# State part of a delta-rule kernel's outputs: one 96-column matmul over both heads of a pair, or one per head over 48 rows

## The chip, the cores and the metric

The kernel runs on one core of one Trainium2 chip. The metric is the time of the device for one execution, in microseconds (us), median of several runs. The engines are TensorE (PE, its weight loads are listed apart as PEld), VectorE (DVE), ScalarE (ACT), GpSimd (POOL) and SyncE (SP, which issues all transfers here).

## What is computed

A delta-rule recurrence over 768 positions for 4 batches of 8 heads with 48 features each, whose output goes through two feed-forward layers (384 to 2048 to 384) with different pointwise functions:

```python
for t in range(S):
    y[:, :, t] = np.einsum('bhd,bhde->bhe', q[:, :, t], state)
    v_old = np.einsum('bhde,bhd->bhe', state, kt)
    state = state + bt[:, :, :, None] * np.einsum('bhd,bhe->bhde', kt, vt - v_old)
x = y.transpose(0, 2, 1, 3).reshape(B * S, H * D)     # 3072 x 384
h = x @ w_in                                          # layer 1
x = np.where(h > 0, h, np.exp(np.minimum(h, 0)) - 1) @ w_out
h = x @ w_in2                                         # layer 2
x = ((a0 + a1*h + a2*h*h + a3*h*h*h) / (1 + |b0|*|h| + |b1|*h*h + 1e-6)) @ w_out2
```

## The kernel before, in words

The recurrence is cut into 12 chunks of 64 positions; two chunks make a window, six windows in all (w = 0 to 5). Within a chunk the 32 pairs of batch and head are handled as 16 pairs of heads: the two heads of a pair lie on partitions 0 to 47 and 64 to 111. A chunk has two halves (hf = 0, 1) of eight head pairs each. Its steps, each a group of PE matmuls in fp32 with copies behind it, are: gp (products of keys and queries, into the masked matrix p), ks (keys times state), a triangular solve in three groups (solve with tp_t, lo, solve with tp_t again), whose result is copied into ub (128 tokens of two batches, 8 pairs, 2 heads, 48 features), yy (the outputs), ku (the update of the state s_bd) and xx (transposes of the outputs into xs, the input of layer 1).

The function yy (line 1007) makes the outputs of one half in one PSUM tile y of 128 x 384. For a chunk that is not the first it issues eight matmuls of the state part, `lhsT` 128 x 64 from kq and `rhs` 128 x 96 from s_bd. s_bd is block diagonal: rows 0 to 47 hold the first head's state in columns 0 to 47, rows 64 to 111 the second's in columns 48 to 95, and the rest is zero. Then it issues eight matmuls of the other part, `lhsT` 128 x 64 from p, `rhs` 128 x 96 from ub, and they are added in PSUM to the first eight. The 64 output rows are tokens; two batches (bl = 0, 1) go to PSUM partitions 0 to 63 and 64 to 127 in turn. One ACT copy brings y to y1 in SBUF (for the first chunk DVE does it). The loads of later chunks (ch_ahead) are called from yy (kq) and ku (kv). xx (line 1030) transposes y1 and copies it into xs; when both chunks of a window are through, split_x (line 911) splits xs into a coarse and a fine part, xh and xl, for layer 1.

Layer 1 and 2 are groups of nine matmuls of 128 x 512 (kind "F" here: H for the first product, O for the second; 2.04 us each). The chain of window w + 1 is issued among the F groups of window w. After window 5 come only F groups, until the end.

The order is not written out by hand. All operations are recorded first (class Recorder), with group kinds for PE (`rc.brk("yy")`). Then `order` (line 329) plans them: `simulate` (line 350) plays the program with estimated durations (PEC, LEAVE, ENTER, PAIR: ns per matmul and ns from the start of one group to the next by kind), margins (SLACK) and tie-breaks drawn from numbers (MIX); the best of eight rounds gives the order in which each engine's instructions are emitted. Each engine then runs its list in that order and waits on semaphores. The times at which the steps are recorded (`chain`, line 921, with SLOTS) set the rank of the groups. The chain's matmuls write to PSUM tiles of the pool pa, three tiles that go round in the order of recording. Where PE would be idle before the first F group, `gaps` (line 314) fills in matmuls without use ("fill").

fp32 matmuls appear in the trace as two MATMUL rows each, with a LDWEIGHTS row each. All recorded operations carry line 191 in the profile (the recorder's emit), so groups are told apart by their tiles.

Of the kernel before, what the change touches and what calls it, by code (L numbers as in the profile page):

```python
# [10 lines left out]
F32 = mybir.dt.float32  # L11
# [3 lines left out]
AF = mybir.ActivationFunctionType  # L15
# [5 lines left out]
D = 48  # L21
NSC = 12
NF = 16
DM = 384
# [7 lines left out]
Q = dict(  # L32
    ma=-200, xo=2.244, pg0=0, pg1=2, ca=0, g1=-72.135, g1d=1.259, t1a=-33.632, t1b=-8, npre=24, ta=-5, tb=4, hd=0.4, c0=-47,
    c0d=1.9, c1=-1.042, c1r=3.6, b1=0.704, c1o=0.919, h0=1.013, h0d=0.5, h1=0.586, h1d=0.462, g2=-7.824,
    g2d=1.116, g3w1=-0.578, g3=-0.806, t2=2.578, t2b=14.166, t3b=9, p=14.315, tm=4, chd=1.061, ws=0.808,
    sx=-0.529, ev=16.5, c5=1.1, c5d=0.4, l5=1.3, wu0=0, wl0=2, wd0=5, wy0=2, wm0=2, wu1=6, wl1=7, wd1=6, wy1=0,
    wm1=6, wk=4, wr=3, wr0=4)
# [135 lines left out]
class Recorder:  # L173
# [58 lines left out]

    def mm(self, out, lhsT, rhs, start, stop):
        kind = self.group.kind
        pitch, lat = PEC[kind]
        self.add("PE", self.nc.tensor.matmul, dict(out=out, lhsT=lhsT, rhs=rhs, start=start, stop=stop), [out], [lhsT, rhs], pitch, lat)

    def transpose(self, out, in_, ident):
# [2 lines left out]
    def act(self, out, in_, **kw):  # L241
        n = out.ids.size
        d = 200 + n * .833 - (30 if in_.base.psum else 0)
        extra = [x for x in kw.values() if isinstance(x, View)]
        d += 90 * len(extra)
        self.add("ACT", self.nc.scalar.activation, dict(out=out, in_=in_, **kw), [out], [in_] + extra, d + self.gap(out, 100), d)
# [4 lines left out]
    def dma(self, out, in_):  # L251
        v = out if isinstance(out, View) else in_
        n = v.ids.size * 4 * (v.part[1] - v.part[0])
        self.add("SP", self.nc.sync.dma_start, dict(out=out, in_=in_), [out], [in_], SLACK["issue"], 2000, n)

# [41 lines left out]

PEC = {
    "F": (226.7, 425), "gp": (206, 475), "ks": (22, 330), "so": (31, 220), "lo": (22, 250), "yy": (85, 262), "ku": (47, 263),
    "xx": (90, 405), "wm": (200, 500), "yt": (33, 260)}  # L300
LEAVE = {"F": 2040, "so": 1062, "lo": 812, "ks": 804, "gp": 914, "ku": 855, "yy": 1471, "xx": 290, "wm": 500, "yt": 1400}
ENTER = {"F": 0, "so": 71, "ks": 71, "xx": -25, "ku": 70, "yy": 20, "gp": -20, "lo": 100, "wm": 50, "yt": 20}
PAIR = {
# [3 lines left out]
SIZE = {"F": 9, "yy": 16, "yt": 48}  # L307
SLACK = {"small": 0, "F": 200, "x": 30, "issue": 500, "rate": 240, "land": 2300, "wait": 1500, "space": 3900, "room": 290, "first": 432, "hold": 200, "jit": 800, "pj": 40}
MIX = [
    (97143513, 1), (80976384, 3), (2505799, 200), (79334811, 200), (73314090, 200), (46793208, 200),  # L310
    (69792616, 200), (68619154, 200), (27185215, 200), (40519137, 200), (78123636, 200), (916308, 200),
]


# [7 lines left out]
def mixed(n):  # L322
    for seed, share in MIX[:0:-1]:
        if draw(seed + 1, n) * share < 1.0:
            return draw(seed, n)
    return draw(MIX[0][0], n)


def order(ops, rounds):
    groups = []  # L330
    for o in ops:
        if o.group is not None and o.group.ops[0] is o:
            o.group.n = o.n
            o.group.rank = o.n + (0 if o.group.kind == "F" else SLACK["pj"] * (mixed(o.n) - .5))
            groups.append(o.group)
            t = 0
            for m in o.group.ops:
                m.off = t
                t += m.pitch
        o.late, o.tie = o.n, mixed(o.n)  # L340
    mine = {o: None for o in ops}
    for o in ops:
        o.deps = {d: k for d, k in o.deps.items() if d in mine}
        for d in o.deps:
            d.succ.append(o)
    best = None
    for _ in range(rounds):
        end = simulate(ops)
        if best is None or end < best[0]:
            best = end, {o: o.start for o in ops}  # L350
        backward(ops, end)
    for o, s in best[1].items():
        o.start = s
    return best[0], sorted(ops, key=lambda o: (o.start, o.n))
# [19 lines left out]
def pe_cost(a, b):  # L374
    return PAIR.get((a, b), LEAVE[a] + ENTER[b])


def simulate(ops):
# [31 lines left out]
    def finish(o, t):  # L410
        nonlocal end
        end = max(end, t)
        for s in o.succ:
# [7 lines left out]
            if g is not None:  # L421
                gready[g] = max(gready[g], r - s.off + SLACK["F" if g.kind == "F" else "small"])
                gleft[g] -= 1
                if not gleft[g]:
                    push(g, gready[g])
            else:
                s.ready = max(s.ready, r + (0 if o.eng == s.eng else SLACK["x"]))
                s.left -= 1
# [3 lines left out]
    def issue(u, t, k):  # L432
# [3 lines left out]
        for o in u.ops:  # L436
            t0 = t + o.off * k + shift
            count += q
            if count > SLACK["first"] - SLACK["room"] + 254.6 * len(usable):
                asked = max(t0 + SLACK["wait"], asked + SLACK["space"])  # L440
                usable.append(asked + 2450)
# [112 lines left out]
def kernel(  # L554
# [16 lines left out]
    nc = tc.nc  # L571
    rc = Recorder(nc)
    mm, act, vector, gpsimd = rc.mm, rc.act, Recorder.Eng(rc, "DVE", nc.vector), Recorder.Eng(rc, "POOL", nc.gpsimd)
    NW = len(WINS)

    def pool(stack, name, bufs, **kw):
        return Pool(rc, stack.enter_context(tc.tile_pool(name=name, bufs=bufs, **kw)), bufs, kw.get("space") is PSUM)
# [18 lines left out]
    ap2 = pool(p1, "ap2", 2)  # L596
    pa = pool(p1, "pa", 3, space=PSUM)
# [23 lines left out]
    p_d = {}  # L621
    s_bd = ap1.tile([128, 16, 2, D], F32, name="s_bd")
# [141 lines left out]
    def ch_ahead(nm):  # L764
        if ch_n[nm] < len(ch_q):
            s, hf = ch_q[ch_n[nm]]
            if nm == "kq":
                t = ap2.tile([128, 8, 128], F32, tag="kq", name="kq")
                rc.dma(out=t, in_=c_kq[s, hf])
            else:  # L770
                t = ap2.tile([128, 8, 96], F32, tag="kv", name="kv")
                rc.dma(out=t, in_=c_kv[s, hf])
            ch_t[nm, s, hf] = t
            ch_n[nm] += 1
# [125 lines left out]
    def warm(dep, n):  # L900
        return
        t = wt.get(0)
        if t is None:
            t = wt[0] = po.tile([128, 512], F32, tag="o0", name="warm")
        rc.brk("wm")
        mm(out=t[0:dep.shape[-1], 0:64 * n], lhsT=dep, rhs=p_d[0][0:dep.shape[0], 0:n].rearrange("p a b -> p (a b)"), start=True, stop=True)
# [14 lines left out]
    def chain(w, slots=SLOTS):  # L921
# [8 lines left out]
        for j, s in enumerate(WINS[w]):  # L930
            st = [dict(), dict()]
# [75 lines left out]
            def yy(hf, j=j, s=s, st=st):  # L1007
                d = st[hf]
                y = pa.tile([128, DM], F32, tag="pa", name="y")
                rc.brk("yy")  # L1010
                if s > 0:
                    for u in range(8):
                        bl, i = u % 2, u // 2
                        mm(out=y[64 * bl:64 * bl + 64, 96 * i:96 * i + 96], lhsT=d["kq"][:, 4 * bl + i, 64 * bl:64 * bl + 64],
                           rhs=s_bd[:, 8 * hf + 4 * bl + i].rearrange("p a b -> p (a b)"), start=(i == 0), stop=False)
                    ch_ahead("kq")
                for u in range(8):
                    bl, i = u % 2, u // 2
                    if w == 0 and u == 4:
                        warm(d["ub"][:, 0, 0, 0:16], Q[f"wm{j}"])  # L1020
                        rc.brk("yy")
                    mm(out=y[64 * bl:64 * bl + 64, 96 * i:96 * i + 96], lhsT=p_d[s][:, 8 * hf + 4 * bl + i],
                       rhs=d["ub"][:, 4 * bl + i].rearrange("p a b -> p (a b)"), start=(s == 0), stop=(s == 0 or i == 3))
                y1 = d["y1"] = ap2.tile([128, DM], F32, tag="y1", name="y1")
                if s == 0:
                    vector.tensor_copy(out=y1, in_=y)
                else:
                    act(out=y1, in_=y, func=AF.Copy)
# [30 lines left out]
            def mk(*fs):  # L1059
                def f():  # L1060
                    for fn, hf in fs:
                        fn(hf)
                return f

            if j == 0:
                xs_d[w] = box
            sl = slots[j]
            items += [
                (sl[0], mk((prep, 0))), (sl[1], mk((prep, 1))), (sl[2], mk((ks, 0), (ks, 1))),
                (sl[3], u1), (sl[4], lo), (sl[5], u2),  # L1070
                (sl[6], mk((yy, 0))), (sl[8], mk((yy, 1))),
                (sl[6] + Q["xo"], mk((xx, 0))), (sl[8] + Q["xo"], mk((xx, 1)))]
            if not last:
                items += [(sl[7], mk((ku, 0))), (sl[9], mk((ku, 1)))]
# [357 lines left out]
    _, first = order(rc.ops, 8)  # L1432
# [94 lines left out]
```

## Time and profile before

| | us |
|---|---|
| median of 3 runs | 1018.04 (1017.91 to 1019.07) |
| the profiled execution | 1017.7 |
| its span, first to last instruction | 1015.9 |
| PE busy | 1001.9 (99%) |
| DVE, ACT, POOL busy | 870.4 (86%), 746.4 (73%), 388.3 (38%) |
| mean granted clock of TensorE | 0.996 |

Busy times are unions over the span. PE rows are pipelined: a MATMUL row lasts longer than the distance to the next one, so distances between starts tell more than durations. The stretch from about 88 to 583 us is layer 1 with the chains of windows 1 to 5 in between; before it lies the chain of window 0, behind it layer 2.

### The profile page before, as it was taken

To read this page: it belongs to the slowest core of one execution; us is meant where nothing else is said; L and a number is where in the kernel's file an instruction comes from. 1 tells how busy PE (TensorE), PEld (TensorE's weight loads), DVE (VectorE), ACT (ScalarE), POOL (GpSimd) and SP (SyncE) were. 2 spreads that over 40 slices of the span, in tenths; PEclk is the share of its full clock that TensorE was granted. 3 is DMA by queue.
4 is the path that set the end of the run, shared out by engine and by line. 5 is a ranking of instruction groups with operands and counts; after the bars stand their busy time and mean duration, and the time that the engine had idled before them with its cause. 6 is when DMAs were issued, how large, how long until landed. Compare 5 with 4: busy or idle time off the path is not lost.

```text
span 1015.9 us, 23204 instructions
## 1 busy us (share of the span) xinstructions
PE 1001.9 (99%) x9234; PEld 833.6 (82%) x9234; DVE 870.4 (86%) x1314; ACT 746.4 (73%) x1467; POOL 388.3 (38%) x287
## 2 busy tenths in 40 slices
PE   8999999999999999999999999999999999999997
PEld 7877888888888888888878888888888888888885
DVE  4999988995997799599875677999999999999996
ACT  4569899877777786778778878677676776766763
POOL 1253655642322223213222235363363553633332
PEclk9999999999999999999999999999999999999999
DMA  9745284217524542642155973001010010000000
GB/s 265 207 139 174 72 239 124 85 62 229 166 76 131 171 166 60 218 152 76 56 173 160 317 244 105 21 10 53 1 63 1 1 63 1 31 1 1 32 1 31
DMA packets 66956, 106.07 MB, mean 104 GB/s; under 512 B 7840, under 2 KB 40736, under 8 KB 66848
## 3 DMA queue, kind: packets, MB, share of 16 engines
q1 hardware_dynamic: 66848, 104.59, 32.7%
q8 instruction: 72, 1.18, 0.5%
q14 instruction: 36, 0.29, 0.1%
HBM read 82.55 MB, written 22.02 MB: 103 GB/s over the span
## 4 chain that ended last, share of the span: by engine, by line
PE 88%; DVE 4%; DMA 3%; ACT 3%; issue 1%; SPq 0%; DVEq 0%; ACTq 0%
PE o L191 37%; PE h L191 18%; PE h_b L191 10%; PE h_a L191 9%; PE cb L191 3%; PE gp L191 3%; PE y L191 2%; PE ku L191 2%; PE ks L191 1%; DMA gin<-g_in 1%; ACT wo L191 1%; PE h_c L191 1%; DMA xg<-g_in 1%; PE xt L191 1%; DVE wo L191 1%; DVE tmp L191 1%
## 5 line engine op out<-in xcount | busy, mean ns | idle before, releaser
L191 POOL TENSOR_TENSOR wor<-wo,wor 128x384 fp32r<-128x384 f32 x96 | 115.6, 1207 | 269.5 <-ACT wor L191 256.7
L191 POOL TENSOR_TENSOR gl<-wo 128x1024 fp32r<-128x1024 f32 x47 | 141.1, 3002 | 191.4 <-DVE wo L191 155.4
L191 PE MATMUL o<-gh,wor 128*128 128x512 f32 x576 | 194.7, 396 | 0.0
L191 PE MATMUL h<-xh,wi 128*128 128x512 f32 x546 | 183.7, 395 | 0.2 <-issue 0.2
L191 ACT ACTIVATE wo<-wo 128x1024 f32<-128x1024 f32 (+3 forms) x224 | 143.0, 671 | 37.2 <-DVE wo L191 34.1
L191 PE MATMUL o<-gh,wo 128*128 128x512 f32 x576 | 139.7, 391 | 0.0
L191 PEld LDWEIGHTS o<-gh,wo 128*128 128x128 f32 x576 | 108.8, 189 | 22.7
L191 PEld LDWEIGHTS o<-gh,wor 128*128 128x128 f32 x576 | 108.1, 188 | 23.1
L191 PEld LDWEIGHTS h<-xh,wi 128*128 128x128 f32 x546 | 102.5, 188 | 22.2 <-ACT pe L191 0.3
L191 PE MATMUL o<-gl,wor 128*128 128x512 f32 x288 | 112.3, 390 | 0.0
L191 PE MATMUL h<-xl,wi 128*128 128x512 f32 x273 | 106.6, 391 | 0.2 <-DVE xl L191 0.2
L191 DVE SCALAR_TENSOR_TENSOR wo<-wo 128x192 int32<-128x192 int32 (+2 forms) x101 | 88.0, 875 | 16.2 <-ACT wo L191 16.1
L191 DVE SCALAR_TENSOR_TENSOR e<-e,pe 128x512 f32<-128x512 f32 x96 | 74.7, 778 | 30.7 <-ACT e L191 30.2
L191 PE MATMUL h_b<-xh,wi 128*128 128x512 f32 x300 | 96.4, 389 | 0.0
L191 DVE TENSOR_TENSOR gl<-e,gh 128x512 fp32r<-128x512 f32 x88 | 73.6, 836 | 18.7 <-ACT gh L191 18.4
L191 PE MATMUL h_a<-xh,wi 128*128 128x512 f32 x276 | 88.9, 389 | 0.0
L191 ACT ACTIVATE wo<-h_b,ab_sb 128x1024 f32<-128x1024 f32 (+1 forms) x52 | 57.6, 1129 | 35.3 <-PE h_b L191 32.8
L191 ACT ACTIVATE e<-h 128x512 f32<-128x512 f32 x91 | 54.4, 598 | 35.5 <-PE h L191 33.9
L191 PE MATMUL o<-gl,wo 128*128 128x512 f32 x288 | 73.8, 391 | 2.0 <-DVE gl L191 2.0
L191 ACT ACTIVATE gh<-e 128x512 fp32r<-128x512 f32 x96 | 60.7, 632 | 15.7 <-PE o L191 10.1
L191 DVE SCALAR_TENSOR_TENSOR gh<-wo,ab_sb 128x1024 fp32r<-128x1024 f32 (+1 forms) x49 | 63.3, 1291 | 9.0 <-ACT wo L191 3.5
L191 PEld LDWEIGHTS h_b<-xh,wi 128*128 128x128 f32 x300 | 56.3, 188 | 11.7
(126 smaller groups left out, 2098.5 us busy)
## 6 DMA issues: line engine op xcount, KB each, us to landing
gin<-g_in SPq DMA_DIRECT2D x69, 192.0 KB, 4.2
kq<-c_kq SPq DMA_DIRECT2D x22, 512.0 KB, 4.7
kv<-c_kv SPq DMA_DIRECT2D x24, 384.0 KB, 5.8
raw<-w_out SPq DMA_DIRECT2D x42, 192.0 KB, 3.0
raw<-w_in SPq DMA_DIRECT2D x34, 192.0 KB, 3.6
o2d<-cs SPq DMA_DIRECT2D x32, 192.0 KB, 2.7
i2d<-cs SPq DMA_DIRECT2D x32, 192.0 KB, 2.3
wi<-i2d SPq DMA_DIRECT2D x16, 384.0 KB, 3.9
```

Source lines behind the costliest of these rows:

```text
L191: fn(**{k: v.real() if isinstance(v, View) else v for k, v in kw.items()})
```

## The change

For windows 1 to 5 a new function yb replaces the two calls of yy: one group (kind "yz") with both halves of the chunk. It has two PSUM tiles, one for each head of a pair, each 128 x (2 halves, 4 pairs, 48). The state part is multiplied per head: `lhsT` 48 x 64 and `rhs` 48 x 48, on partitions from 0 or from 64, 32 matmuls a chunk where there were 16 of 128 x 64 by 128 x 96. The other part has `rhs` 128 x 48 per head, 32 matmuls where there were 16 with 96 columns. Four ACT copies of 128 x 192 (half and head) bring the two tiles to the two y1 tiles, where two copies of 128 x 384 did. Both kq loads of the chunk are called behind the group's matmuls. Window 0 keeps yy; its second call is now recorded at the first one's place, and the break within its group is gone. The planner gets constants for "yz", a lookup by the number of rows, other margins and other numbers for its tie-breaks.

```diff
--- before.py
+++ after.py
@@ -232,7 +232,7 @@
 
     def mm(self, out, lhsT, rhs, start, stop):
         kind = self.group.kind
-        pitch, lat = PEC[kind]
+        pitch, lat = PEC.get((kind, lhsT.part[1] - lhsT.part[0]), PEC[kind])
         self.add("PE", self.nc.tensor.matmul, dict(out=out, lhsT=lhsT, rhs=rhs, start=start, stop=stop), [out], [lhsT, rhs], pitch, lat)
 
     def transpose(self, out, in_, ident):
@@ -297,18 +297,19 @@
 
 PEC = {
     "F": (226.7, 425), "gp": (206, 475), "ks": (22, 330), "so": (31, 220), "lo": (22, 250), "yy": (85, 262), "ku": (47, 263),
-    "xx": (90, 405), "wm": (200, 500), "yt": (33, 260)}
-LEAVE = {"F": 2040, "so": 1062, "lo": 812, "ks": 804, "gp": 914, "ku": 855, "yy": 1471, "xx": 290, "wm": 500, "yt": 1400}
-ENTER = {"F": 0, "so": 71, "ks": 71, "xx": -25, "ku": 70, "yy": 20, "gp": -20, "lo": 100, "wm": 50, "yt": 20}
+    "xx": (90, 405), "yz": (22, 262), ("yz", 128): (43, 262),  "wm": (200, 500), "yt": (33, 260)}
+LEAVE = {"F": 2040, "so": 1062, "lo": 812, "ks": 804, "gp": 914, "ku": 855, "yy": 1471, "yz": 2200, "xx": 290, "wm": 500, "yt": 1400}
+ENTER = {"F": 0, "so": 71, "ks": 71, "xx": -25, "ku": 70, "yy": 20, "yz": 20, "gp": -20, "lo": 100, "wm": 50, "yt": 20}
 PAIR = {
-    ("F", "so"): 2131, ("F", "gp"): 2140, ("F", "lo"): 2263, ("F", "yy"): 2266, ("F", "ks"): 2225, ("F", "xx"): 2049,
+    ("F", "so"): 2131, ("F", "gp"): 2140, ("F", "lo"): 2263, ("F", "yy"): 2266, ("F", "yz"): 2266, ("F", "ks"): 2225, ("F", "xx"): 2049,
     ("F", "ku"): 2230, ("F", "yt"): 2266, ("ks", "ks"): 704, ("yy", "yy"): 1371, ("yy", "ku"): 1371, ("yy", "xx"): 1421, ("yy", "gp"): 1435,
     ("ku", "ku"): 755, ("ku", "yy"): 755, ("xx", "ku"): 450, ("xx", "ks"): 477, ("yt", "yt"): 1365}
 SIZE = {"F": 9, "yy": 16, "yt": 48}
-SLACK = {"small": 0, "F": 200, "x": 30, "issue": 500, "rate": 240, "land": 2300, "wait": 1500, "space": 3900, "room": 290, "first": 432, "hold": 200, "jit": 800, "pj": 40}
+SLACK = {"small": 150, "F": 100, "x": 15, "issue": 500, "rate": 240, "land": 2000, "wait": 2000, "space": 3900, "room": 290, "first": 432, "hold": 200, "jit": 800, "pj": 0}
 MIX = [
-    (97143513, 1), (80976384, 3), (2505799, 200), (79334811, 200), (73314090, 200), (46793208, 200),
-    (69792616, 200), (68619154, 200), (27185215, 200), (40519137, 200), (78123636, 200), (916308, 200),
+    (52832997, 1), (92410015, 200), (32312298, 200), (83369229, 200), (2388703, 200), (46334073, 60),
+    (81258500, 60), (36371637, 200), (64931058, 200), (82440171, 200), (11413780, 60), (11428128, 200),
+    (90112574, 200), (20237250, 20),
 ]
 
 
@@ -1016,11 +1017,33 @@
                     ch_ahead("kq")
                 for u in range(8):
                     bl, i = u % 2, u // 2
-                    if w == 0 and u == 4:
-                        warm(d["ub"][:, 0, 0, 0:16], Q[f"wm{j}"])
-                        rc.brk("yy")
                     mm(out=y[64 * bl:64 * bl + 64, 96 * i:96 * i + 96], lhsT=p_d[s][:, 8 * hf + 4 * bl + i],
                        rhs=d["ub"][:, 4 * bl + i].rearrange("p a b -> p (a b)"), start=(s == 0), stop=(s == 0 or i == 3))
+                y_out(y, d, s)
+
+            def yb(_, s=s, st=st):
+                rc.brk("yz")
+                ys = [pa.tile([128, 2, 4, D], F32, tag="pa", name="y") for _ in range(2)]
+                for i in range(4):
+                    for bl in range(2):
+                        for hf, d in enumerate(st):
+                            for h in range(2):
+                                rs = slice(64 * h, 64 * h + D)
+                                mm(out=ys[h][64 * bl:64 * bl + 64, hf, i], lhsT=d["kq"][rs, 4 * bl + i, 64 * bl:64 * bl + 64],
+                                   rhs=s_bd[rs, 8 * hf + 4 * bl + i, h], start=(i == 0 and hf == 0), stop=False)
+                for hf, d in enumerate(st):
+                    for i in range(4):
+                        for h in range(2):
+                            for bl in range(2):
+                                mm(out=ys[h][64 * bl:64 * bl + 64, hf, i], lhsT=p_d[s][:, 8 * hf + 4 * bl + i], rhs=d["ub"][:, 4 * bl + i, h],
+                                   start=False, stop=(hf == 1 and i == 3))
+                for hf, d in enumerate(st):
+                    ch_ahead("kq")
+                    y1 = d["y1"] = ap2.tile([128, DM], F32, tag="y1", name="y1")
+                    for h in range(2):
+                        act(out=y1.rearrange("p (i h d) -> p i h d", h=2, d=D)[:, :, h], in_=ys[h][:, hf], func=AF.Copy)
+
+            def y_out(y, d, s):
                 y1 = d["y1"] = ap2.tile([128, DM], F32, tag="y1", name="y1")
                 if s == 0:
                     vector.tensor_copy(out=y1, in_=y)
@@ -1068,7 +1091,7 @@
             items += [
                 (sl[0], mk((prep, 0))), (sl[1], mk((prep, 1))), (sl[2], mk((ks, 0), (ks, 1))),
                 (sl[3], u1), (sl[4], lo), (sl[5], u2),
-                (sl[6], mk((yy, 0))), (sl[8], mk((yy, 1))),
+                (sl[6], mk((yy, 0), (yy, 1)) if w == 0 else mk((yb, 0))),
                 (sl[6] + Q["xo"], mk((xx, 0))), (sl[8] + Q["xo"], mk((xx, 1)))]
             if not last:
                 items += [(sl[7], mk((ku, 0))), (sl[9], mk((ku, 1)))]
```

## Rows read from the trace of the kernel before

**Rows 1.** The page, part 1: busy us (share of span) x instructions

```profile
PE 1001.9 (99%) x9234; PEld 833.6 (82%) x9234; DVE 870.4 (86%) x1314; ACT 746.4 (73%) x1467; POOL 388.3 (38%) x287
```

**Rows 2.** Busy us of each engine, PEclk, DMA share, GB/s, one stretch

```profile
265.00:353.00 88.00, 87.76 (x1229) 73.77 (x1232) 75.34 (x156) 68.58 (x165) 25.04 (x21) 1.00 0.47 147
```

**Rows 3.** Timeline of PE from 267 us: start us, us, engine, operation, count

```profile
267.07 0.88 PE L191 MATMUL y<-s_bd,kq 128*64 128x96 f32 x16
267.78 0.83 PE L191 MATMUL y<-ub,p 128*64 128x96 f32 x16
268.44 0.83 PE L191 MATMUL y<-s_bd,kq 128*64 128x96 f32 x16
...
269.86 0.55 PE L191 MATMUL xt<-cm_sb,y 128*128 128x128 f32 x3
270.34 1.65 PE L191 MATMUL ku<-ub,kv 128*48 128x48 f32 x64
271.92 0.55 PE L191 MATMUL xt<-cm_sb,y 128*128 128x128 f32 x3
...
277.38 1.58 PE L191 MATMUL ks<-s_bd,kq 128*32 128x48 f32 x128
278.89 0.50 PE L191 MATMUL h<-xh,wi 128*128 128x512 f32 x1
```

**Rows 4.** Timeline of PE from 235 us

```profile
235.96 0.88 PE L191 MATMUL y<-s_bd,kq 128*64 128x96 f32 x16
...
237.43 1.16 PE L191 MATMUL gp<-gin 96*128 96x128 f32 x8
...
239.28 0.85 PE L191 MATMUL y<-s_bd,kq 128*64 128x96 f32 x16
...
240.71 1.16 PE L191 MATMUL gp<-gin 96*128 96x128 f32 x8
```

**Rows 5.** Timeline of PE from 250 us

```profile
257.32 1.13 PE L191 MATMUL cb<-R,tp_t 32*32 32x48 f32 x64
258.38 0.50 PE L191 MATMUL o<-gh,wor 128*128 128x512 f32 x1
...
260.65 0.88 PE L191 MATMUL cb<-R,lo 32*32 32x48 f32 x64
261.46 0.50 PE L191 MATMUL h<-xh,wi 128*128 128x512 f32 x1
```

**Rows 6.** By tile (y, ku, cb): duration ns min/median/max, first and last start

```profile
L191 PEld LDWEIGHTS y<-s_bd,kq x352: 132/137/138, 79.7 to 536.7; 128*64 128x64 f32 x176
L191 PE MATMUL y<-s_bd,kq x352: 246/246/297, 79.7 to 536.8; 128*64 128x96 f32 x176
...
L191 PE MATMUL ku<-ub,kv x704: 206/208/243, 65.0 to 510.1; 128*48 128x48 f32 x176
...
L191 PEld LDWEIGHTS cb<-R,tp_t x1408: 126/146/149, 73.9 to 532.3; 32*32 32x32 f32 x176
...
L191 PEld LDWEIGHTS cb<-R,lo x704: 101/105/105, 75.9 to 527.0; 32*32 32x32 f32 x176
```

**Rows 7.** ACT by form: x count | busy us, mean ns | idle before

```profile
L191 ACT ACTIVATE cs<-ce 128x192 fp32r<-128x192 f32 x64 | 21.9, 362 | 3.4 <-DVE ce L191 2.6 <-DMA o2d<-cs 0.4 <-DVE t L191 0.3
...
L191 ACT ACTIVATE y<-y 128x384 f32<-128x384 f32 x22 | 10.9, 495 | 2.3 <-PE y L191 2.2
```

**Rows 8.** Tile kq from 260 to 285 us: its loads

```profile
L191 SPq DMA_DIRECT2D kq<-c_kq x2: 334/334/334, 268.0 to 269.3; - x2
...
DMA to landing us min/median/max: 3.5/3.9/4.2
```

**Rows 9.** Timeline of PE from 338 us

```profile
339.70 1.58 PE L191 MATMUL ks<-s_bd,kq 128*32 128x48 f32 x128
341.51 0.39 PE L191 MATMUL h<-xh,wi 128*128 128x512 f32 x1 [0.24 <-issue]
```

**Rows 10.** Timeline of DVE from 272 us

```profile
276.28 0.67 DVE L191 TENSOR_TENSOR xl<-xs,xh 128x512 fp32r<-128x512 f32 x1
```


## Prediction, made before the changed kernel ran

> **What bounds the kernel now.** I read the shares of the engines first: TensorE (PE) is busy 1001.9 of 1015.9 us [rows 1]. A share can hide stages, so the next view is the stretches: between 265 and 353 us, one pass over a window with its two chunks, PE is busy 87.76 of 88 us at a granted clock of 1.00, ScalarE (ACT) 68.58 and VectorE 75.34 [rows 2]. So here every us that PE is given or spared moves the end one for one, and the other engines have room. Then the timeline of PE alone, where I take the time from the start of one row to the start of the next, because pipelined rows overlap. The second chunk of a window issues its two y groups in one block, 267.07 to 269.86 = 2.79 us [rows 3]; the first chunk splits them, 235.96 to 237.43 and 239.28 to 240.71, 1.47 + 1.43 = 2.90 us [rows 4]. There are five blocks and five splits in windows 1 to 5, the only ones that the new function serves. So all that the change can touch directly is 5 x 2.79 + 5 x 2.90 = 28.5 us.
>
> **What one matmul step costs.** Each fp32 matmul of the code is two MATMUL rows, each with its weight load. Two limits have to be told apart: the columns that stream (N) and the columns of the weights that are loaded (M). Moving columns: the y parts have 16 rows on two column tiles, 8 steps in 267.78 to 268.44 = 0.66, 82 ns for N = 96 [rows 3]. The solve's lo part has 64 rows on four tiles, 16 steps, 260.65 to 261.46 = 0.81 [rows 5], some 42 ns a step at N = 48 once the tail is taken off. Weights: the first matmul of a group, whose load nothing covers, is longer than the median one by 297 - 246 = 51 ns at M = 64 and 243 - 208 = 35 ns at M = 48 [rows 6]; that is 0.8 or 0.7 ns a column. So y today streams for 82 ns and hides a load of 51. After the change it streams for 42 ns against the same load of 51, because the 64 tokens stay the weights' columns.
> Does the longer of the two set the step? One pair of rows says so. The solve through tp_t has the same 64 rows, tiles and N as lo and differs in its weights, which are read with a stride: their load takes 146 ns in place of 105 [rows 6], and the group 257.32 to 258.38 = 1.06 in place of 0.81 [rows 5], 0.25 / 16 = 16 ns a step more, about 58 in all. A load of 137 ns (M = 64) lies between those, nearer to 146. I take 55 ns a step, with 42 (loads hidden after all) and 58 as the ends.
>
> **The sum for the new group.** State part: 32 matmuls, 64 rows, on four 64x64 tiles, 16 steps; lo gives 0.81, the tp_t solve 1.06; at 55 ns 0.81 + 16 x 0.013 = 1.02. Both rows contain the pause for the change of tile shape behind them, which the group needs too before its second part. Second part: 32 matmuls (twice as many as before, N 48 in place of 96, all 128 rows), 64 rows on two tiles, 32 steps. The ku pair is exactly that with M = 48: 270.34 to 271.92 = 1.58 [rows 3], of which a step is about 45 (its load and its stream are equally long); 10 ns more a step for M = 64 gives 1.58 + 0.32 = 1.90. Together 2.92. The ends: 0.81 + 1.58 = 2.39 if loads stay hidden, 1.06 + 1.58 + 32 x 0.013 = 3.06 at 58 ns.
> Against the rows of before: 5 x (2.92 - 2.79) + 5 x (2.92 - 2.90) = +0.75 us; with 3.06 it is +2.2, with 2.39 it is -4.6. The halved work in the state part is given back by the doubled weight loads of the other.
>
> **What moves.** Today the first half's copy to y1 runs beside the second half's matmuls, and a transpose follows at 269.86, at once [rows 3]. Now no copy can start before the whole group ends, and there are four of 128x192 in place of two of 128x384: about 0.36 each by the nearest form against 0.495 [rows 7], 1.45 in place of 0.99. So ACT gains 0.46 us a chunk, 4.6 in all, hidden under its idle time (19 of 88 us [rows 2]). Queued behind them on ACT are that window's exp, split and conversion pieces; they have the same cover. The first transpose needs two of the copies, so some 0.8 us pass behind the group. The three PSUM tiles of that pool go round in order, the second chunk's first transpose stands ahead of its ku groups, and two tiles are now held at once, so PE puts one wide group there. That group is work that has to be done anyway; what it costs is one more entry, about 0.1 us (an exposed load of weights, as at the head of any group), for five chunks +0.5. In the first chunk ku can follow at once: nothing.
> SP: both kq loads of a chunk are now called after the group, but each waits only for the readers of its own tile, and all those lie in the state part. Today they issue at 268.0 and 269.3 and land 3.9 us later [rows 8]; the reader is the ks group at 277.38 [rows 3]. Cost nothing; if that 4 us of cover were gone, PE would wait. The kv loads stay with ku.
> Instructions: 64 more matmul rows and 64 more loads a chunk. After a dense ks group PE once waited 0.24 us for "issue" [rows 9]; between none and one such wait a chunk that is 0 to +2.4; I take +0.3, as most dense groups of before show none.
> The planner's constants and tie-breaks change too, so every order may be redrawn. In the stretch of rows 2 PE has 0.24 us left to win; a bad order could cost as much as those waits. I take 0, within 1 us either way, the start-up included. Window 0 keeps the old matmuls: 0.
> Sum: 0.75 + 0.5 + 0.3 = +1.55 us. The profiled execution took 1017.7 (span 1015.9, 1.8 around it), 0.34 under the median of the three runs; 1017.7 + 1.55 = 1019.25, and on the scale of the median **1019.6 us**. About 0.2% (2 us) is what a measurement here can tell from no change.
>
> **Rivals.** (A) The forecast, own range 1017 to 1022.
> (B) Weight loads stay hidden, the step is 42 ns: 2.39 a chunk, -4.6 + 0.8 = -3.8, **1014.2 us**, faster. For it: lo and ku run at their streaming rate. Against: both have loads no longer than their streams, and tp_t, the one group with a longer load, is slower. The Trainium skill, TensorEngine Tiling (Array Packing), Theoretical Speedup, sides with B: a small contraction gives up to 2x, and it names no limit by weight loads. No row of before has 64x64 tiles to show it.
> (C) Two heads whose tiles lie in the same columns don't run side by side. The ks, lo and solve groups all use four different column ranges, so no row shows two row tiles over one range. Then the state part has 32 steps, 32 x 0.055 + 0.13 = 1.9, 0.87 more in ten chunks: +8.7 + 1.55, **1028.3 us**, slower. Against: the heads go to separate PSUM tiles, and lo and the solve do run 32-row tiles together.
> The Trainium skill, TensorE: Matmul & The Clock Gate, Measured speedup vs the span model, gives 3.07 for four row tiles; by that ratio the state part would be an estimated 1.02 x 4 / 3.07 = 1.33 and the sum 3 us more than mine, and no run here shows it.
> (D) The late y1 reaches the window's end. Behind the last transpose come the split's pieces, the last xl at 276.28 + 0.67 [rows 10]; the next window's first matmul starts at 278.89 [rows 3], 1.9 us of slack. Group, wide group, transposes and ku put the last transpose about 2.2 us later. Above 1.9 us PE waits: at 2.2 it is 0.3 a window, with a second wide group in between some 2.3. Taking 1 us in five windows: +5, **1024.6 us**, slower. For it: the slack is as small as the delay. Against: the planner sees this wait and can shift the wide groups.
>
> **How the numbers follow.** Chances: A 0.55, B 0.15, C 0.10, D 0.15, a luckier order 0.05. The range 1012.5 to 1026 leaves out C, the slow tail of D and the fast tail of B, under 2 in 10. Faster by over 0.2% (below 1016.0): B and the luckier order, 0.20. Slower by over 0.2% (above 1020.1): C, D and a good quarter of A, 0.40. Within: 0.40.
>
> **What would show it.** In the profile after: the y group of windows 1 to 5, start to next start, 2.9 to 3.1 (A), 2.4 (B) or 3.8 (C); its second part about 1.9; the first matmul of the group longer than the median by about 50 ns; a wide group between y and the first transpose of the second chunk; at a window's end no PE wait for xl (A) or one (D). I am wrong if the second part takes 1.6, or if PE's time in the start-up moves by over 1 us.

## The result, and the profile after

The change made the kernel slower: 1025.3 us (1023.52 to 1026.89) against 1017.97 in the same comparison, ratio 1.008, 95% interval 1.0063 to 1.0097. That is +7.3 us by the medians and some 8 by the ratio, where +1.6 and "no change that can be told" was forecast. The profiled execution took 1025.49, its span 1023.7; it is compared below with the one of before (span 1015.9), +7.8.

The page, part 1, and the stretch that answers to [rows 2]:

```profile
span 1023.7 us, 24543 instructions
...
PE 1009.5 (99%) x9890; PEld 839.5 (82%) x9890; DVE 873.3 (85%) x1314; ACT 745.3 (73%) x1487; POOL 383.7 (37%) x287
```

```profile
265.00:353.00 88.00, 88.00 (x1243) 73.70 (x1245) 69.55 (x140) 66.57 (x163) 23.95 (x21) 1.00 0.46 142
```

PE has 656 rows more (640 of them the second matmuls per head) and is busy 7.6 us longer; inside the windows it was full before and is full now. So the question is only which PE time was added. I took it from the PE timeline of both traces, from the first wide group on, as distances from the start of one group to the start of the next, added up by kind:

| | before | after | difference |
|---|---|---|---|
| start of the first wide group | 87.92 | 92.67 | +4.75 |
| ten y groups of windows 1 to 5 | 28.58 | 31.51 | +2.93 |
| wide groups up to 583 us, above 2.04 us each | 12.28 | 13.88 | +1.60 |
| ks, gp, ku, xt after the first wide group | 66.04 | 64.36 | -1.68 |
| the last two wide groups, to the last PE row | 7.71 | 7.79 | +0.08 |
| start of the last PE row | 1011.20 | 1018.86 | +7.66 |

The -1.68 has 0.98 in ks, nearly all because one half of a ks group (0.82) now stands ahead of the first wide group and no longer behind it. Set against the 4.75, the start-up is some 3.8 us late and the windows give the other 3.8.

The granted clock of TensorE does not set these two traces apart: its mean is 0.996 in both. Both have 3.4 us at 0.50, the lower of the two levels (1.2 GHz), in the last two wide groups (1007.9 to 1011.3 before, 1015.0 to 1018.4 after), behind a stop of PE of 2.0 us for gl, and 3.4 us in the start-up (in the trace of before PE had been busy 2.53 of the 4.00 us from 55 to 59). This second stretch, before and after, with the columns of [rows 2]:

```profile
59.00:62.40 3.40, 3.40 (x70) 2.46 (x69) 2.35 (x4) 2.79 (x9) 1.98 (x3) 0.50 0.48 139
```

```profile
59.30:62.70 3.40, 3.40 (x77) 2.48 (x70) 3.21 (x5) 1.85 (x6) 2.02 (x4) 0.50 0.43 111
```

**The second chunk of a window**, the stretch that answers to [rows 3] (timeline of PE):

```profile
269.51 1.18 PE L191 MATMUL y<-s_bd,kq 48*64 48x48 f32 x64
270.62 2.07 PE L191 MATMUL y<-ub,p 128*64 128x48 f32 x64
272.62 0.50 PE L191 MATMUL o<-gh,wor 128*128 128x512 f32 x1
...
274.83 0.49 PE L191 MATMUL xt<-cm_sb,y 128*128 128x128 f32 x3
275.25 1.65 PE L191 MATMUL ku<-ub,kv 128*48 128x48 f32 x64
...
281.79 0.50 PE L191 MATMUL h<-xh,wi 128*128 128x512 f32 x1
```

The state part takes 269.51 to 270.62 = 1.11, the second part 270.62 to 272.62 = 2.00, the group 3.11 in place of 2.79. A wide group (272.62 to 274.83) stands between it and the first transpose, as forecast. The next window's first H, 281.79, comes without a wait.

**The first chunk of a window** (timeline of PE, the same chunk of the cycle as [rows 4]):

```profile
329.15 1.22 PE L191 MATMUL y<-s_bd,kq 48*64 48x48 f32 x64
330.31 2.07 PE L191 MATMUL y<-ub,p 128*64 128x48 f32 x64
332.31 1.16 PE L191 MATMUL gp<-gin 96*128 96x128 f32 x8
333.22 0.47 PE L191 MATMUL o<-gh,wor 128*128 128x512 f32 x1
...
335.48 0.93 PE L191 MATMUL ku<-ub,kv 128*48 128x48 f32 x32
336.34 1.16 PE L191 MATMUL gp<-gin 96*128 96x128 f32 x8
337.33 0.49 PE L191 MATMUL xt<-cm_sb,y 128*128 128x128 f32 x3
337.58 0.48 PE L191 MATMUL h<-xh,wi 128*128 128x512 f32 x1
...
339.81 0.93 PE L191 MATMUL ku<-ub,kv 128*48 128x48 f32 x32
340.66 1.16 PE L191 MATMUL gp<-gin 96*128 96x128 f32 x8
341.65 0.49 PE L191 MATMUL xt<-cm_sb,y 128*128 128x128 f32 x3
341.90 0.48 PE L191 MATMUL o<-gh,wor 128*128 128x512 f32 x1
```

Here the old order had y, gp, ku, y, gp, xt, ku in one piece, then a wide group, then gp and xt. Now wide groups stand at 333.22, 337.58 and 341.90, so each ku has one before it, and from y to the last xt there are two wide groups in place of one. Counted over the windows, the entries (wide groups with a group of another kind behind them) rise from 60 to 67: four in the first chunks (the last window has no gp, and no more entries than before) and three in the second. What is scarcer can be read from the program: gp and ku take their PSUM tile from the same three, the group holds two of them, and the four copies come only behind it (timeline of ACT):

```profile
332.31 1.00 ACT L191 ACTIVATE y<-y 128x192 f32<-128x192 f32 x4 [0.74 <-PE y L191]
```

That this puts the wide group just before ku is not shown: in e7_yb_fit below, the same function in another order, ku follows gp at once in three of four windows.

**The group's rows by themselves** (tile y, second chunk: duration min/median/max in ns):

```profile
L191 PE MATMUL y<-s_bd,kq x64: 218/218/253, 269.5 to 270.5; 48*64 48x48 f32 x64
L191 PEld LDWEIGHTS y<-ub,p x64: 133/138/139, 270.6 to 272.4; 128*64 128x64 f32 x64
L191 PE MATMUL y<-ub,p x64: 221/222/257, 270.6 to 272.5; 128*64 128x48 f32 x64
L191 ACT ACTIVATE y<-y x4: 325/334/352, 272.6 to 273.3; 128x192 f32<-128x192 f32 x4
```

The first matmul of the second part is longer than the median by 257 - 222 = 35 ns, the loads of 64 columns are as long as in [rows 6], and the copies take 0.334 each. The prediction's sign for a load that nothing covers was about 50 ns, so it came out smaller; the median row is itself longer, 222 for the 208 of ku with its 48 columns of weights [rows 6].

**The start-up.** Tile kv between 50 and 90 us, before and after: the loads of the second chunk's kv, the POOL scaling, and R = kv - ks on DVE (duration min/median/max, first and last start; the first of each kind is the one to compare):

```profile
L191 SPq DMA_DIRECT2D kv<-c_kv x4: 328/378/384, 66.4 to 86.5; - x4
L191 POOL TENSOR_TENSOR kv<-kv,n_t x3: 863/897/939, 70.3 to 89.6; 128x384 f32<-128x384 f32 x3
...
L191 DVE TENSOR_TENSOR R<-kv,ks x2: 540/540/541, 72.1 to 73.6; 128x384 f32<-128x384 f32 x2
```

```profile
L191 SPq DMA_DIRECT2D kv<-c_kv x3: 382/389/793, 68.4 to 89.0; - x3
...
L191 POOL TENSOR_TENSOR kv<-kv,n_t x2: 827/828/829, 74.2 to 75.6; 128x384 f32<-128x384 f32 x2
L191 DVE TENSOR_TENSOR R<-kv,ks x2: 542/548/553, 75.1 to 76.6; 128x384 f32<-128x384 f32 x2
```

```profile
75.10 0.55 DVE L191 TENSOR_TENSOR R<-kv,ks 128x384 f32<-128x384 f32 x1 [1.28 <-POOL kv L191]
```

The first kv load is issued 2.0 us later (68.4 for 66.4), POOL starts on it 3.9 us later (74.2 for 70.3), and DVE, in its fixed order, stands 1.28 us for it before R (last of these fences). R runs at 75.10 where it ran at 72.05. So 1.28 of these 3.05 us are the wait for kv; the other 1.8 were lost earlier, for the first chunk's ku group of window 0, ahead of any use of these tiles, is as late (timeline of PE, before and after):

```profile
65.04 1.98 PE L191 MATMUL ku<-ub,kv 128*48 128x48 f32 x63
```

```profile
66.83 1.98 PE L191 MATMUL ku<-ub,kv 128*48 128x48 f32 x63
```

None of these instructions belongs to the new function: windows from 1 on use it, this is window 0. What changed for them is the order, that is, the margins, the tie-breaks and the place at which window 0's second y is recorded.

### The profile page after: what moved, and what is told of

Read it like the earlier page. It is cut to its first block, busy times and chain, and to the rows that moved or that the text cites. A ratio compares the mean times of both kernels' runs of the same rounds, so it can differ in the third digit from the quotient of the medians.

```text
span 1023.7 us, 24543 instructions
## 1 busy us (share of the span) xinstructions
PE 1009.5 (99%) x9890; PEld 839.5 (82%) x9890; DVE 873.3 (85%) x1314; ACT 745.3 (73%) x1487; POOL 383.7 (37%) x287
## 3 DMA queue, kind: packets, MB, share of 16 engines
q8 instruction: 78, 1.28, 0.5%
## 4 chain that ended last, share of the span: by engine, by line
PE 91%; DVE 6%; DMA 1%; issue 1%; ACT 1%; SPq 0%; POOL 0%; ACTq 0%; DVEq 0%; POOLq 0%
PE o L191 38%; PE h L191 19%; PE h_b L191 10%; PE h_a L191 9%; PE gp L191 4%; PE y L191 3%; PE cb L191 3%; PE ku L191 2%; DVE tmp L191 1%; PE ks L191 1%; PE h_c L191 1%; DVE tt L191 1%; DVE wo L191 1%; PE xt L191 1%; DMA wo<-g_in 1%
## 5 line engine op out<-in xcount | busy, mean ns | idle before, releaser
L191 ACT ACTIVATE wo<-wo 128x192 f32<-128x192 f32 (+3 forms) x224 | 142.8, 671 | 50.0 <-DVE wo L191 47.1
L191 DVE SCALAR_TENSOR_TENSOR wo<-wo 128x192 int32<-128x192 int32 (+2 forms) x101 | 92.9, 924 | 15.6 <-ACT wo L191 15.5
L191 DVE SCALAR_TENSOR_TENSOR e<-e,pe 128x512 f32<-128x512 f32 x96 | 74.1, 773 | 31.4 <-ACT e L191 31.0
```

The lines of the kernel that those rows point to most:

```text
L191: fn(**{k: v.real() if isinstance(v, View) else v for k, v in kw.items()})
```

## The experiments

Two questions: what sets the 3.11 us (weight loads, W, or the stream, S), and what moved the rest (the redrawn order, O, or the function itself, Y).

### Only the constants: e1_consts

```diff
-SLACK = {"small": 0, "F": 200, "x": 30, ...
-MIX = [(97143513, 1), (80976384, 3), ...
+SLACK = {"small": 150, "F": 100, "x": 15, ...      # as in the changed kernel
+MIX = [(52832997, 1), (92410015, 200), ...
```

> The kernel before with the changed kernel's margins (SLACK) and tie-breaks (MIX) and nothing else. Theory O (half of the loss is the redrawn order: the first wide group starts at 92.67 us in place of 87.92, of which 0.8 to 1.0 is a ks group moved ahead of it): start-up some 3.9 us later here too, the windows unchanged within 1 us, 1021.9 us in all. Rival Y (the new function, with its second call of window 0 recorded earlier, does all of it): 1018.0, the first wide group at 88.

Measured: 1023.65 us (ratio 1.0069, interval 1.0051 to 1.0088; before 1016.39 in that comparison). Slower by 7.3 with the old y groups untouched. The same tile and columns as above, then PE:

```profile
L191 SPq DMA_DIRECT2D kv<-c_kv x4: 370/383/390, 68.4 to 89.2; - x4
...
L191 POOL TENSOR_TENSOR kv<-kv,n_t x2: 827/830/833, 74.1 to 75.5; 128x384 f32<-128x384 f32 x2
L191 DVE TENSOR_TENSOR R<-kv,ks x2: 542/548/553, 75.0 to 76.4; 128x384 f32<-128x384 f32 x2
```

```profile
92.11 0.51 PE L191 MATMUL h<-xh,wi 128*128 128x512 f32 x1
```

The start-up is that of the changed kernel almost to the row: kv at 68.4, 74.1 and 75.0, the first wide group at 92.11. So Y falls for the start-up: it comes with the constants, 3.4 us of it (92.11 - 87.92, less the half ks group of 0.82). The granted clock has no part in it: this trace has 1.00 from 59.0 to 62.5, where the other two have the lower level, and is late all the same. The forecast of O was short by 2 us: the rest lost some as well (wide groups up to 583 us 14.18 above 2.04 each for 12.28 before, and 1.47 more between there and the last two, where before has 0.01). That this comes of draws made for another program is likely by e9 below, not shown by this run.

### Only the function: e2_yb_old_consts

```diff
 # the changed kernel, with before's
+SLACK = {"small": 0, "F": 200, "x": 30, ...
+MIX = [(97143513, 1), (80976384, 3), ...
```

> The changed kernel with the margins and tie-breaks of before. Theory O: the new function alone costs ten groups of 3.11 for 28.6 us of the old ones, +2.9, and about seven more entries of wide groups, +0.9 net: 1021.8 us, with the first wide group near 88. Rival Y: 1025.3, first wide group near 92.7. Second rival: this order was never fitted to the new groups, so the start-up or the windows come out worse than either, above 1026.

Measured: 1033.51 us (ratio 1.0156, 1.0124 to 1.0188). The second rival came true. Its ten groups cost 31.72 us, as in the changed kernel; the first wide group starts at 90.66. The rest are mostly waits of PE that neither kernel has (waits: total us, times, longest):

```profile
PE ks L191 <- issue: 3.9, 3, 2.1
...
PE h L191 <- ACT xh L191: 1.8, 1, 1.8
PE h L191 <- ACT e L191: 1.7, 1, 1.7
```

The granted clock is at 0.50 from 286.3 to 289.7 and from 480.8 to 484.2 as well, the first time from the end of a stop of PE of 1.55 us inside a ks group, and two wide groups there take 1.40 and 1.16 us longer than 2.04. So an order that was not chosen for the program at hand cost more here than the function does, and this run can't price the function.

### Two arbitrary orders of the old program: e6_draw1, e6_draw4

```diff
 # the kernel before
-MIX = [(97143513, 1), (80976384, 3), ... twelve draws ...]
+MIX = [(11111111, 1)]            # e6_draw4: (44444444, 1)
```

> The kernel before, its twelve draws (MIX) replaced by one arbitrary number: same operations, margins and prices, another order. Theory O (an order that was not fitted costs several us whatever the function): 1021 to 1028, with the start-up or waits in the windows as the place. Rival (the order is worth little; the margins of the changed kernel were what hurt in the run with its constants): 1016 to 1019.

> A second arbitrary number in the same place. Theory O: 1021 to 1028 again, differing from the first draw by a few us. Rival: 1016 to 1019.

Measured: 1020.78 (ratio 1.0024, 1.001 to 1.0037) and 1022.73 (1.0053, 1.003 to 1.0075), before 1017.39. Same operations, prices and margins, +3.4 and +5.3 us. The first wide group starts at 90.57 and 89.19 (87.92 before), and in e6_draw4 the wide groups up to 583 us lie 15.14 above 2.04 each (12.28 before). Of that, 1.66 are one group at 125.84 in a stretch at the lower level (granted clock 0.51 from 125.5 to 129.0), behind a stop of PE of 1.43 us for a load of wo. O holds: the second lies in its range, the first just under it (by the ratio it is only 2.4 us).

### Weights or stream: e4_m48 and e4_n24

Both keep the changed kernel's operations and order and leave out part of the second part's result.

```diff
 # e4_m48: 48 of 64 tokens
-out=ys[h][64 * bl:64 * bl + 64, hf, i], lhsT=p_d[s][:, 8 * hf + 4 * bl + i]
+out=ys[h][64 * bl:64 * bl + 48, hf, i], lhsT=p_d[s][:, 8 * hf + 4 * bl + i, 0:48]
 # e4_n24: 24 of 48 columns
-out=ys[h][64 * bl:64 * bl + 64, hf, i], ... rhs=d["ub"][:, 4 * bl + i, h]
+out=ys[h][64 * bl:64 * bl + 64, hf, i, 0:24], ... rhs=d["ub"][:, 4 * bl + i, h, 0:24]
```

> The changed kernel, the second part's weights cut from 64 to 48 columns (16 of 64 tokens get no second part), same number of matmuls, same 48 moving columns, same order. Theory W (a step lasts as long as the weight load): the second part falls from 2.00 to about 1.58, as the ku pair, the median load row from 138 to 125 ns, the kernel by 4.2 us to 1021.1. Rival S (a step lasts as long as the stream or the issue of a matmul): 2.00 and 1025.3 as before.

> The changed kernel, the second part's moving columns cut from 48 to 24 (half of each output row gets no second part), same weights, same number of matmuls, same order. Theory W (a step lasts as long as the load of 64 columns of weights): the second part stays at about 2.0 us and the kernel at 1025. Rival S (the stream sets the step): the step halves or falls to the issue distance, the second part falls to 1.0 to 1.3, the kernel by 7 to 10 us to 1015 to 1018.

Measured: e4_m48 1021.39 us (1.0042, 1.0022 to 1.0061), e4_n24 1023.93 us (1.0062, 1.0041 to 1.0083). Timeline of PE in the same chunk, e4_m48 first:

```profile
270.75 1.65 PE L191 MATMUL y<-ub,p 128*48 128x48 f32 x64
272.32 0.50 PE L191 MATMUL o<-gh,wor 128*128 128x512 f32 x1
```

```profile
270.75 2.05 PE L191 MATMUL y<-ub,p 128*64 128x24 f32 x64
272.73 0.50 PE L191 MATMUL o<-gh,wor 128*128 128x512 f32 x1
```

A quarter of the weights' columns away: second part 270.75 to 272.32 = 1.57. Half of the stream away: 270.75 to 272.73 = 1.98, for 2.00 in the changed kernel. The loads themselves (tile y of e4_m48, same chunk) took 125 ns in the median for 138, as W had it:

```profile
L191 PEld LDWEIGHTS y<-ub,p x64: 119/125/125, 270.7 to 272.1; 128*48 128x48 f32 x64
```

So W is shown for the second part and S refuted: with 64 columns of weights the step lasts as long as their load, and it doesn't matter whether 48 or 24 columns stream past them. Fewer columns of weights also mean fewer rows of output, but the two solve groups of [rows 5, 6] differ in the load alone and differ in the same way. For the state part nothing was varied; that its 16 steps go by the load too is argued from their like length.

### Joining without splitting: e3_merge

```diff
 # in yb: one tile per half, both heads at once
-ys[h][64 * bl:64 * bl + 64, hf, i] <- kq[rs, ...] x s_bd[rs, ..., h]        # 48 x 48, twice as many
+ys[hf][64 * bl:64 * bl + 64, 96 * i:96 * i + 96] <- kq[...] x s_bd[...]     # 128 x 96
-("yz", 128): (43, 262)   ...   "yz": 2200
+("yz", 128): (82, 262)   ...   "yz": 2742
```

> The changed kernel with the old matmuls in the new group: both halves of a chunk in one group, one PSUM tile for each half, 96 columns, two ACT copies; the planner is told 2.74 us for the group in place of 2.2. Tells the split per head from the joining of halves. If the split costs 0.32 us a chunk (3.11 against 2.79): group 2.79, total 3.2 us below the changed kernel, 1022.1. If the joining (late copies, more entries) is the larger part, 1024 to 1025. A redrawn order can add up to 4 either way, so the group and the entries are read from its trace.

Measured: 1032.68 us (1.0158, 1.0127 to 1.0189), far off. The group itself (timeline of PE), and the largest of its waits:

```profile
376.69 1.59 PE L191 MATMUL y<-s_bd,kq 128*64 128x96 f32 x32
378.06 1.54 PE L191 MATMUL y<-ub,p 128*64 128x96 f32 x32
379.53 0.50 PE L191 MATMUL o<-gh,wor 128*128 128x512 f32 x1
```

```profile
285.84 0.87 PE L191 MATMUL ks<-s_bd,kq 128*32 128x48 f32 x60
289.12 0.28 PE L191 MATMUL ks<-s_bd,kq 128*32 128x48 f32 x4 [2.41 <-issue]
```

The joined group of old matmuls takes 376.69 to 379.53 = 2.84, so of the 0.32 that the new group is longer than the old pair of the second chunk, 0.27 are the split per head and 0.05 the joining. The total is again an order that wasn't fitted: one ks group alone stops for 2.41 us, and behind it the granted clock is 0.50 from 289.9 to 293.3. For what joining does to the rest of the kernel this run is inconclusive.

### The planner told the right price, and the draws fitted anew: e5_priced, e7_yb_fit, e9_old_margins_fit, e8_old_fit

```diff
 # e5_priced: the changed kernel
-"yz": (22, 262), ("yz", 128): (43, 262)   ...   "yz": 2200
+"yz": (34, 262), ("yz", 128): (58, 262)   ...   "yz": 3100
 # e7_yb_fit: e5_priced with 60 draws found by search on the planner's own estimate
 # e9_old_margins_fit: e1_consts with 28 such draws (the old function)
 # e8_old_fit: the kernel before with 37 such draws
```

> The changed kernel with the planner told what its group costs on the chip (34 ns a state matmul, 58 ns a matmul of the second part, 3.10 us for the group) and nothing else changed; the draws stay. If the wrong price alone made the order bad, the loss shrinks: the ten groups stay at 3.11 each but start-up and entries come back, 1021 to 1022. If the draws are what counts (they were fitted to the wrong price, and any new price reshuffles all), it is no better and may be worse: 1025 to 1031.

> The changed kernel with the prices of e5_priced and draws fitted anew to them by the planner's own estimate, 40 minutes of search. If the order was the larger part of the loss and can be won back, only the function's own cost stays: ten groups of 3.11 for 28.6 us (+2.9) and entries (+0.9), so 3 to 5 us over e9 below, 1020 to 1022. If the function itself costs the whole 7, it stays at 1024 to 1026.

> The kernel of e1_consts (old function, the changed kernel's margins) with draws fitted anew in the same way and time. Theory O: the 6 to 7 us that e1_consts lost come back, 1016 to 1018. Rival (the margins were what hurt): 1021 to 1024 still.

> The kernel before with more search on its own draws, nothing else. About 1 us is what the planner still sees: 1016 to 1018, at best just faster than before; if its estimate is not good to 1 us, anything from 1015 to 1021.

Measured: e5_priced 1024.48 (1.0073, 1.0052 to 1.0094; before 1017.39). In one comparison, before 1017.47: e7_yb_fit 1023.54 (1.0055, 1.0037 to 1.0072), e9_old_margins_fit 1018.76 (1.0026, 1.0011 to 1.004), e8_old_fit 1017.37 (1.0007, 0.9994 to 1.002).

e5 and e7 fall between what their rivals forecast, e9 just above what O forecast, e8 where it was expected. e9 wins back 4 to 6 of the 7 us that e1_consts lost, with the same margins: most of that loss was the draws, and 1.3 (by the medians) to 2.6 (by the ratio) are left, of the margins or of one search that found no better. e7 does not win back much: fitted for its true price the new function stays at +6.1, and 4.8 above e9 by the medians, 3.0 by the ratios; e9 has the same margins and as long a search. Between the traces of these two the ten y groups differ by 31.66 - 28.60 = 3.06 us and the wide groups' excess by 1.21, which is 4.3 of the 5.1 us between their spans (wide groups up to 583 us: 13.56 and 12.35). At the end e7 loses 1.07 us that are not the function's: its last two wide groups take 7.26 for 6.19, with a granted clock of 0.50 from 1014.8 to 1018.2, where e9 has 1.00 until its last PE row. Shorter ks, xt and gp groups give some of it back. The start-ups are within 0.3 us once a half ks group (0.82) ahead of it in e7 is taken off, though e7 has the lower level from 59.1 to 62.5 and e9 from 34.5 to 37.9:

```profile
91.15 0.50 PE L191 MATMUL h<-xh,wi 128*128 128x512 f32 x1
```

```profile
90.04 0.50 PE L191 MATMUL h<-xh,wi 128*128 128x512 f32 x1
```

In the first chunk e7 has ku behind gp at once, without a wait of PE (timeline of PE; the four copies run from 239.06 to 240.06):

```profile
239.06 1.16 PE L191 MATMUL gp<-gin 96*128 96x128 f32 x8
240.14 0.93 PE L191 MATMUL ku<-ub,kv 128*48 128x48 f32 x32
241.00 1.16 PE L191 MATMUL gp<-gin 96*128 96x128 f32 x8
```

A wide group then stands before the first transpose instead, and the entries are 67 as in the changed kernel, for 59 in e9.

The right price alone (e5) gives 1024.48 where the changed kernel had 1025.3, in another comparison: no difference that can be told. Neither is e7 against the changed kernel (intervals 1.0037 to 1.0072 and 1.0063 to 1.0097 overlap). No version beats the kernel before; e8 equals it.

## Why the prediction was wrong, point by point

**What bounds the kernel: right.** PE is full in the windows, and its time moved the end: e4_m48 took 4.1 us from the ten y groups, and the time fell by 3.9. ACT's extra copies (4 x 0.334 for 2 x 0.495) cost nothing by their length.

**One step lasts as long as its weight load: right, and the size at the upper end.** Forecast 55 ns with 58 as the end; e4_m48 and e4_n24 show the mechanism for the second part, and 2.00 us for 32 steps less the tail is 58. The pair of rows of the solve, which differ in the load alone [rows 5, 6], was the right place to read it. Term by term: state part 1.02 forecast, 1.11 measured (1.06, the tp_t solve's own time, was nearer); second part 1.90 forecast, 2.00 measured; the group 2.92 against 3.11, outside the range of 2.39 to 3.06. Together with three groups that were longer still (3.16, 3.26 and 3.40) that is +2.9 where +0.75 was forecast: 2.2 us short. Rival B falls with it. The rule quoted beside B (the Trainium skill, TensorEngine Tiling (Array Packing), Theoretical Speedup: up to 2x for a small contraction) speaks of the state part: there the trace has 1.11 for 1.37, a gain of 1.2x. The split also halved the columns of the second part, which has no small contraction, and the two parts came to 3.11 in place of 2.84 for the joined old ones.

**Row tiles over one column range: rival C refuted.** 64 rows in 1.11 us is four tiles at work; two would have taken 1.9. The estimate of 1.33 for this part, by the ratio in the Trainium skill (TensorE: Matmul & The Clock Gate, Measured speedup vs the span model), was too high by 0.22; my 1.02 was too low by 0.09.

**What moves: the second chunk right in kind, the first too low.** "In the first chunk ku can follow at once: nothing" failed by its "nothing". I let ku take the tile of the solve and forgot that gp, recorded in between, takes a turn in the same ring, so that ku needs a tile of the group, and with it the late copies. That ku can follow at once holds even so where the order has it (e7); but a first chunk with a gp has one more entry in the changed kernel, whichever group it stands before. Entries rose by 4 in the first chunks and 3 in the second, where I had 5 in the second alone. The wide groups' excess rose by 1.60, of which 0.7 came back (xt 0.86 and gp 0.21 shorter, ku 0.37 longer), net 0.9; I had 0.5. Rival D did not come true: the next window's H never waits for xl.

**"Any order may be redrawn ... I take 0, within 1 us either way, the start-up included": this failed most.** The start-up alone is 3.8 us late, which the prediction had named as a sign of being wrong, and 3.4 of it come without the new function (e1_consts). I priced the new order by what PE had left to win in one window and by one wait, and looked at no row of the start-up, where PE runs fill matmuls and the chain goes through DVE, POOL and the kv loads. Two arbitrary orders of the old program cost 3.4 and 5.3 us (2.4 and 5.4 by the ratios): 1 us was too narrow by a factor of two to five. The centre of 0 was too low too: both arbitrary orders lost, and more search on the draws of before (e8) won nothing. It had to be a term of its own, above zero, and a rival on the slow side.

**The sum.** Forecast 1.55 = 0.75 + 0.5 + 0.3; measured 7.3 to 7.8 = 3.8 (start-up) + 2.9 (groups; the 0.3 for instructions would be in their three longer ones, if anywhere) + some 0.9 (entries, net of shorter small groups). That 1025.3 lies within 1012.5 to 1026 is luck: the slow end stood there for D, which did not happen. At equally fitted orders (e7 against e9) the function costs 3 to 5 us, two to three times the forecast, with the right sign. How the changed kernel's remaining 2 to 4 us split between its margins (1 to 3 by e9), draws fitted to a price of 2.20 for a group of 3.11, and chance is not settled: the intervals overlap.

## What to carry to other kernels

Before a matmul is cut into narrower ones, compare the load of its weights with what will stream past them: here 96 columns hid a load of 64 and 48 didn't, and the cut gave back more than row tiling had won (2.00 for 1.47 in the second part, 1.11 for 1.37 in the state part). Where a planner draws the order, every edit redraws it: price that as a loss of the size that an arbitrary draw costs (2 to 5 us here), look for it in the stage where several engines wait in turn, and compare functions only at orders fitted for each, with the granted clock of each trace beside them. A tile that is held longer can be felt by the next group in the ring, whichever kind that is: count the turns of the ring before calling a tile free.

## What the runs showed of the hardware

Two row tiles over the same columns, with outputs in two PSUM tiles, run side by side: 64 matmul rows of 48x64 by 48 in 1.11 us, and the state part alone did gain from the split, 1.11 for 1.37 (0.71 + 0.66 in two groups before, 1.37 joined in e3_merge). With half its columns (24 for 48) a stream of matmuls took the same time, 1.98 us for 64 rows, at 64 columns of weights. And a dense group can stop in its middle for 2.41 us with no releaser in the trace (e3_merge, 60 of 64 ks rows out); the trace has a packet of the instruction queue in that gap, but that the group waited for it was not tested. Behind that stop the granted clock fell from 1.00 to 0.50, and a wide group took 3.53 us in place of 2.04.
